# First batch's stage-1 banks emptied by two engines on opposite halves, w loaded amid x, the left-over column loaded early

## The chip, the cores and the metric

The kernel runs on one core of a Trainium2 chip. The core has TensorE (PE in the rows; its weight loads are PEld), VectorE (DVE), ScalarE (ACT), GpSimd (POOL) and SyncE (SP, which issues most DMAs). The metric is the device time of one run in microseconds (us). The time before is 1080.98 us, the median of three runs (1078.39 to 1082.65).

## The reference

`x` has 8 batches of 2496 positions of 256 channels. Each batch goes through a real FFT along the positions, a complex product with `w_r` and `w_i`, a soft threshold and an inverse FFT. The result, 19968 rows of 256, goes through a mixture of eight experts, of which each row takes one.

```python
X = np.fft.rfft(x, axis=1)
Yr = Xr @ w_r - Xi @ w_i + b_r
Yi = Xr @ w_i + Xi @ w_r + b_i
Yr = np.sign(Yr) * np.maximum(np.abs(Yr) - lam, 0.0)      # Yi alike
y = np.fft.irfft(Y, n=x.shape[1], axis=1)
# then per row: skip_score = x @ w_skip; e_idx = argmax(x @ w_gate)
y[mask] = gate_w[mask, None] * (np.maximum(xc[mask] @ w1[e], 0.0) @ w2[e])
out[do_compute] = xc + y
```

## The kernel before

2496 is 39 times 64, so the FFT is done in two stages of matrix products with constant tables. Stage 1 is the 39-point transform: for the position `n2` of 64 it multiplies 39 inputs by `fwd1`. Stage 2 (`fwd2_step`, L485) is a 64-point transform for each of 20 frequencies `k`. `mix` (L515) multiplies by w, and `inv2_step` and `out_tasks` do the way back. The main loop at L900 takes one frequency of one batch per step: 8 batches of 20 steps. In it a step of one batch's stage 2 stands beside units of the next batch's stage 1, and every instruction's place on its engine follows from the order in which the code emits it: engines take their instructions in that order, and wait on semaphores.

Products in the main loop are made of three single-pass products, so each operand is split into a high part (a ScalarE copy to fp32r: `xh`, `fh`, `wh`) and a low part (the rest, by VectorE or GpSimd: `xl`, `fl`, `wl`).

Batches 1 to 7 pass through memory between the stages: stage 1 (`a1_unit`, `a1_mm`, tile `pa`) writes `z`, then `zs` in memory, and `load_r` (L475) reads it back as `r`. Position 63 is left over by the division of 63 positions into units; it is done for three batches at a time from a small tile `xq` (`a1_left_prep`, L453).

Batch 0 takes a shorter way, `a1_first` (L393). Its `x` comes laid out as 43 groups of 128 columns (`x0`), in six DMAs of seven groups and a small one (`x_e`). TensorE multiplies each group by `fwd1` in full fp32, four groups to a PSUM bank (`pd`): 11 banks, of which six buffers exist. Every bank has 128 partitions; the lower half holds channels 0 to 127, the upper half channels 128 to 255. For each half h, ScalarE copies the first 20 frequencies (real parts) to partitions 0 to 63 of `r0`, then VectorE copies the other 19 to partitions 64 to 127 (L409, L410). `r0` is what stage 2 of batch 0 reads.

After `a1_first` come the splits of `fwd1` (L886) and of the three matrices in `wst` (w_i - w_r, w_i + w_r, w_r; L887), and then three steps of `fwd2_step` ahead of the main loop. Before everything, `spin` (L323) runs five products on zeros on TensorE.

DMAs that SP issues use eight semaphores in rotation: an issue waits until the DMA eight places earlier has landed. Their order on SP is shown with the change.

```python
            for h in range(2):                                    # L407
                rows, d = slice(64 * h, 64 * h + 64), slice(128 * h + 3 * g0, 128 * h + 3 * g0 + w)
                nc.scalar.activation(r0[0:64, :, d], src[rows, :K1, :w], AF.Copy)
                nc.vector.tensor_copy(r0[64:128, 1:, d], src[rows, K1:, :w])
```

Of the kernel before, what the change touches and what calls it, by code (L numbers as in the profile page):

```python
# [37 lines left out]
G0 = 43  # L38
# [11 lines left out]
GROUPS = ((0, 1, 2), (3, 4, 5), (6, 7))  # L50
# [245 lines left out]
def fft_and_route(tc, a, out, zs, xs, kp, pp, keep_, outer):  # L296
    nc = tc.nc
# [7 lines left out]
    KG = 5  # L305
# [30 lines left out]
    fwd2 = cp.tile([128, K1, 128], F32, name="fwd2")  # L336
# [11 lines left out]
    def setup_a():  # L348
        nc.sync.dma_start(bias[:, 0], a["b_r"].unsqueeze(0).broadcast_to((128, D)))
        nc.sync.dma_start(bi, a["b_i"].unsqueeze(0).broadcast_to((128, D)))  # L350
        nc.vector.memset(neglam, -LAM)
# [38 lines left out]
        mm(pa[:np_, :n], f1l[:np_, :np_], xh[:np_, :n], start=False, stop=True)  # L390
        return pa

    def a1_first(loads):  # L393

        at = lambda g: next((t, g - g0) for t, g0, g1 in loads if g0 <= g < g1)
        for g0 in range(0, G0, 4):
            gs = range(g0, min(g0 + 4, G0))
            w = min(3 * len(gs), 128 - 3 * g0)
            pd = bank(pp, f"pd{g0}")
            for i, g in enumerate(gs):  # L400
                t, gg = at(g)
                mm(
                    pd[:, P1 * i : P1 * i + P1], t[:, 128 * gg : 128 * gg + 128], fwd1,
                    start=True, stop=True, skip_group_check=True,
                )
            src = pd[:, : P1 * len(gs)].rearrange("p (w k) -> p k w", k=N1)
            for h in range(2):  # L407
                rows, d = slice(64 * h, 64 * h + 64), slice(128 * h + 3 * g0, 128 * h + 3 * g0 + w)
                nc.scalar.activation(r0[0:64, :, d], src[rows, :K1, :w], AF.Copy)  # L409
                nc.vector.tensor_copy(r0[64:128, 1:, d], src[rows, K1:, :w])  # L410
        for q in range(K1 // KG):
            rt[0, q] = r0[:, KG * q : KG * q + KG]

    def a1_tasks(b):

        tasks = []

        def unit(c, o, no, first, last):
            st = {}

            def prep():
                if first and (b, c) not in xraw:
                    load_x(b, c)
                st["t"] = a1_unit(b, c, o, no, xraw[b, c])

# [25 lines left out]
        return tasks

    def a1_left_prep(bs, st):  # L453
        np_ = N1 * len(bs)
        t = xp.tile([P1, D], F32, name=f"xq{bs[0]}", tag="xq", bufs=1)
        nc.sync.dma_start(t[:np_], a["xq"][bs[0] : bs[-1] + 1].rearrange("b n d -> (b n) d"))
        xh = xp.tile([P1, 2 * D], F32R, name=f"xh{bs[0]}q", tag="xh", bufs=3)
        xl = xp.tile([P1, 2 * D], F32R, name=f"xl{bs[0]}q", tag="xl", bufs=3)
        nc.scalar.activation(xh[:np_, :D], t[:np_], AF.Copy)
        nc.gpsimd.tensor_tensor(out=xl[:np_, :D], in0=t[:np_], in1=xh[:np_, :D].bitcast(F32), op=ALU.subtract)  # L460
        st["t"] = xh, xl, D
# [23 lines left out]
    def fwd2_step(b, k):  # L485
        r = rt[b, k // KG]
        kk = k % KG
        kp_ = 128 if k else 64
        pb = bank(pp, f"pb{b}_{k}")[:, : 2 * 128].rearrange("p (h c) -> p h c", h=2)
        for h in range(2):  # L490
            mm(pb[:, h], r[:kp_, kk, 128 * h : 128 * h + 128], fwd2[:kp_, k], start=True, stop=True)  # L491
        p = k // 2
        if k % 2 == 0:
            xb[b, p] = [sp.tile([128, 2, 3, 2, 64], F32R, name=f"f{n}{b}_{p}", tag="f" + n, bufs=2) for n in "hl"]
            sb[b, p] = sp.tile([128, 2, 2, 64], F32, name=f"s{b}_{p}", tag="sum", bufs=2)
        (xh, xl), s = xb[b, p], sb[b, p]
        for_k = lambda t: t[:, :, 0:2, k % 2, :]
        src = pb.rearrange("p h (c j) -> p h c j", c=2)
        nc.scalar.activation(for_k(xh), src, AF.Copy)  # L499
        im = sp.tile([128, 2, 64], F32, name=f"im{b}_{k}", tag="im", bufs=2)  # L500
        nc.scalar.activation(im, src[:, :, 1], AF.Copy)  # L501
        nc.vector.tensor_tensor(out=for_k(xl), in0=src, in1=for_k(xh).bitcast(F32), op=ALU.subtract)  # L502
        nc.vector.tensor_tensor(out=s[:, :, k % 2], in0=src[:, :, 0], in1=im, op=ALU.subtract)
        if k % 2:
            def split_sum():
                nc.scalar.activation(xh[:, :, 2], s, AF.Copy)
                nc.gpsimd.tensor_tensor(out=xl[:, :, 2], in0=s, in1=xh[:, :, 2].bitcast(F32), op=ALU.subtract)  # L507

            defer(*D_SUM, split_sum)
# [342 lines left out]
    def a1_step(q, ahead=2):  # L852
# [6 lines left out]
        if n >= ahead or not q:  # L859
            if prepped:  # L860
                prepped.pop(0)[1]()

    loads = []
    for g0, g1 in ((0, 14), (14, 28), (28, 42), (42, G0)):
        t = sp.tile([P1, CH * RW], F32, name=f"x0_{g0}", tag="row", bufs=3) if g1 < G0 else xp.tile([P1, D], F32, name="x0_e", tag="xq", bufs=1)
        n = 128 * (g1 - g0)
        for c in range(0, n, 128 * CH):
            c1 = min(c + 128 * CH, n)
            nc.sync.dma_start(t[:, c:c1], a["x0"][:, 128 * g0 + c : 128 * g0 + c1])
        loads.append((t, g0, g1))  # L870
    nc.sync.dma_start(fwd2[:, 0:KG], a["fwd2"][:, 0:KG])
    wr = wst[:, 2]
    nc.sync.dma_start(wr, a["w_r"].rearrange("(h p) e -> p h e", p=128))
    nc.sync.dma_start(wi, a["w_i"].rearrange("(h p) e -> p h e", p=128))
    load_x(1, 0)
    nc.gpsimd.tensor_tensor(out=wst[:, 0], in0=wi, in1=wr, op=ALU.subtract)
    nc.gpsimd.tensor_tensor(out=wst[:, 1], in0=wi, in1=wr, op=ALU.add)
    setup_a()
    nc.sync.dma_start(fwd2[:, KG : 2 * KG], a["fwd2"][:, KG : 2 * KG])
    load_x(1, 1)  # L880
    nc.sync.dma_start(inv2[:, 0:KG], a["inv2"][:, 0:KG])
    load_x(1, 2)
# [200 lines left out]
```

## Time and profile before

| | |
|---|---|
| median of three runs | 1080.98 us |
| the profiled execution, its own time | 1079.93 us |
| its span in the trace | 1078.2 us |
| TensorE busy | 1038.8 us, 96% of the span |
| VectorE busy | 718.6 us, 67% |
| ScalarE busy | 619.0 us, 57% |
| GpSimd busy | 437.5 us, 41% |
| moved by DMA | 132.33 MB, mean 123 GB/s |

The rows of a timeline give the start, the length (from the first to the end of the last where several are merged, with xN), the engine, the line, the operation with output and inputs, and in brackets the idle time before it and what ended it. TensorE's granted clock stands in the views by stretches as a share: 1.00 is 2.4 GHz, 0.50 is 1.2 GHz.

### The profile page before, as it was taken

The numbers are of one execution on the slowest core, as the hardware profiler recorded it, in microseconds if no ns is written. First come the engines' busy times: TensorE is split into PE (matmuls) and PEld (weight loads), VectorE is DVE, ScalarE is ACT, GpSimd is POOL, SyncE is SP. The second block draws the span as 40 slices with busy tenths as digits, with TensorE's granted clock in tenths as the row PEclk, the third lists the DMA queues.
The fourth block names the chain that finished last, engine by engine and source line by source line (L and its number), as shares of the span: only waits on it lengthen the run. The fifth ranks groups of instructions, "written<-read, shape, count | busy, mean of one in ns | idle before, by whom it ended". The sixth has DMA issues, their size and how long they took to land. (4 is left out here: it accounts for less than half of the span.)

```text
span 1078.2 us, 27343 instructions
## 1 busy us (share of the span) xinstructions
PE 1038.8 (96%) x8572; PEld 1017.0 (94%) x8572; DVE 718.6 (67%) x2025; ACT 619.0 (57%) x1811; POOL 437.5 (41%) x599
## 2 busy tenths in 40 slices
PE   7979999999999999999989989999999999999997
PEld 6879999999999999999989989999999999999997
DVE  4677787987888878789986444454545455465443
ACT  5758887788887878877875333243323343244232
POOL 1514177383665836734457522222222222222222
PEclk8989999999999999999999999999999999999999
DMA  8653656666567556463345641131413123141111
GB/s 274 187 145 85 173 147 176 181 170 183 145 166 225 138 169 167 115 180 93 115 117 146 221 114 52 39 113 47 123 39 117 46 70 96 39 130 46 39 39 40
DMA packets 83184, 132.33 MB, mean 123 GB/s; under 512 B 12504, under 2 KB 61578, under 8 KB 83080
## 3 DMA queue, kind: packets, MB, share of 16 engines
q1 hardware_dynamic: 68085, 110.45, 36.8%
q0 software_dynamic: 14864, 20.55, 6.2%
q8 instruction: 52, 0.85, 0.4%
q14 instruction: 53, 0.43, 0.1%
q10 hardware_dynamic: 130, 0.05, 0.0%
HBM read 69.77 MB, written 72.07 MB: 132 GB/s over the span
## 5 line engine op out<-in xcount | busy, mean ns | idle before, releaser
L224 ACT ACTIVATE hh<-ph 128x256 fp32r<-128x256 f32 x304 | 118.0, 388 | 289.5 <-PE ph L222 269.2
L648 POOL DMA_INDIRECT xs<-row,pos x168 | 169.1, 1007 | 62.5 <-issue 28.0
L225 DVE SCALAR_TENSOR_TENSOR hl<-ph,hh 128x256 fp32r<-128x256 f32 x304 | 128.2, 424 | 59.1 <-ACT hh L224 58.9
L545 DVE SCALAR_TENSOR_TENSOR y<-pm,rl 64x256 f32<-64x256 f32 x320 | 134.2, 419 | 4.4 <-issue 0.2
L525 PE MATMUL pm<-wh,fh 128*128 128x256 f32 x480 | 110.9, 313 | 14.9 <-DVE y L545 8.0
L507 POOL TENSOR_TENSOR fl<-s,fh 128x256 fp32r<-128x256 f32 x80 | 58.7, 734 | 162.8 <-issue 80.3
L243 DVE SCALAR_TENSOR_TENSOR ot<-pos,xres 128x256 f32<-128x256 f32 x76 | 33.3, 480 | 109.4 <-PE ph L222 95.4
L491 PE MATMUL pb<-fwd,r 128*128 128x128 f32 (+1 forms) x640 | 100.6, 281 | 4.2 <-ACT r L409 4.2
L222 PE MATMUL ph<-bxh,wb1h 128*128 128x256 f32 x352 | 98.8, 281 | 2.7 <-PEq L1079 2.7
L525 PEld LDWEIGHTS pm<-wh,fh 128*128 128x128 f32 x480 | 76.7, 193 | 23.2 <-DVE y L545 8.2
L222 PE MATMUL ph<-bxh,wb1l 128*128 128x256 f32 x352 | 98.2, 279 | 0.0
L222 PE MATMUL ph<-bxl,wb1h 128*128 128x256 f32 x352 | 98.2, 279 | 0.0
L561 PE MATMUL pi<-inv,y 128*128 128x128 f32 (+1 forms) x640 | 97.0, 274 | 0.3 <-ACT z L432 0.3
L525 PE MATMUL pm<-wh,fl 128*128 128x256 f32 x480 | 96.6, 283 | 0.5 <-DVE fl L502 0.5
L525 PE MATMUL pm<-wl,fh 128*128 128x256 f32 x480 | 96.9, 283 | 0.1
L491 PEld LDWEIGHTS pb<-fwd,r 128*128 128x128 f32 (+1 forms) x640 | 88.5, 195 | 7.8 <-ACT r L409 4.6
L499 ACT ACTIVATE fh<-pb 128x256 fp32r<-128x256 f32 x160 | 61.1, 382 | 59.2 <-PE pb L491 57.4
L256 POOL DMA_INDIRECT out<-ot,idx x78 | 78.1, 1002 | 28.6 <-issue 27.6
L382 POOL TENSOR_TENSOR xl<-xr,xh 117x512 fp32r<-117x512 f32 x63 | 81.0, 1287 | 21.1 <-ACT xh L380 20.2
L561 PEld LDWEIGHTS pi<-inv,y 128*128 128x128 f32 x640 | 84.7, 191 | 0.7 <-ACT z L432 0.5
L580 DVE TENSOR_TENSOR tl<-pt,th 117x266 fp32r<-117x266 f32 x168 | 71.2, 428 | 16.8 <-ACT th L579 16.5
L502 DVE TENSOR_TENSOR fl<-pb,fh 128x256 fp32r<-128x256 f32 x160 | 67.8, 424 | 16.9 <-ACT im L501 13.0
(222 smaller groups left out, 3189.4 us busy)
## 6 DMA issues: line engine op xcount, KB each, us to landing
out<-row SPq DMA_DIRECT2D x72, 273.0 KB
xr<-in_xc SPq DMA_DIRECT2D x21, 819.0 KB
zs<-z SPq DMA_DIRECT2D x63, 273.0 KB
r<-zs SPq DMA_DIRECT2D x49, 320.0 KB
ws<-in_moe_w SPq DMA_DIRECT2D x28, 512.0 KB
xbuf<-xs SPq DMA_DIRECT2D x41, 258.0 KB, 2.8
xs<-row,pos POOLq DMA_INDIRECT x168, 4.7
x<-in_x SPq DMA_DIRECT2D x6, 409.5 KB
```

The source lines that it names most:

```text
L222: self.nc.tensor.matmul(p, l_[:, c, fc], r_[:, c, :], start=n == 0, stop=n == 5)
L224: self.nc.scalar.activation(self.hh[:, f, :], p, AF.Relu)
L225: self.nc.vector.scalar_tensor_tensor(out=self.hl(f), in0=p, scalar=0.0, in1=self.hh[:, f, :].bitcast(F32), op0=ALU.max, op1=ALU.subtract)
L256: si = gp.indirect_dma_start(out=self.out, out_offset=bass.IndirectOffsetOnAxis(ap=self.idx[:, r : r + 1], axis=0), in_=ot[:, r, :], in_of ...
L382: eng.tensor_tensor(out=xl[:, :n], in0=v, in1=xh[:, :n].bitcast(F32), op=ALU.subtract)
L491: mm(pb[:, h], r[:kp_, kk, 128 * h : 128 * h + 128], fwd2[:kp_, k], start=True, stop=True)
L502: nc.vector.tensor_tensor(out=for_k(xl), in0=src, in1=for_k(xh).bitcast(F32), op=ALU.subtract)
L525: mm(out, flat(l_, h, j), r_[:, j, h], start=start and n == 0, stop=n == 5, skip_group_check=True)
L545: nc.vector.scalar_tensor_tensor(out=y[64 * c : 64 * c + 64], in0=t[rows, c], scalar=LAM, in1=r[rows, c], op0=ALU.add, op1=ALU.min)
L561: mm(pi[:, h, :nn], y[:, 128 * h : 128 * h + 128], inv2[:, k, :nn], start=True, stop=True)
L580: nc.vector.tensor_tensor(out=tl[:np_], in0=pt[:np_], in1=th[:np_].bitcast(F32), op=ALU.subtract)
L648: si = nc.gpsimd.indirect_dma_start(out=xs, out_offset=bass.IndirectOffsetOnAxis(ap=pos[pl, o : o + 1], axis=0), in_=row[pl, o, :], in_off ...
```

## The change

In each bank ScalarE and VectorE now start on opposite halves and then change over, so that both are at work in one bank. w is loaded after the second of the six parts of x, and xq for batches 0 to 2 behind the first loads (for the later groups one chunk earlier). `fwd1` is split before the banks. `wst` is joined amid the banks and split in three pieces (ScalarE and GpSimd): one after bank 8, two between the first steps of stage 2. Two products on zeros follow the last bank.

```diff
-    def a1_first(loads):
+    def a1_first(loads, more):
...
-            for h in range(2):
-                rows, d = slice(64 * h, 64 * h + 64), slice(128 * h + 3 * g0, 128 * h + 3 * g0 + w)
-                nc.scalar.activation(r0[0:64, :, d], src[rows, :K1, :w], AF.Copy)
-                nc.vector.tensor_copy(r0[64:128, 1:, d], src[rows, K1:, :w])
+            n = g0 // 4
+            for turn in range(2):
+                def part(h):
+                    return slice(64 * h, 64 * h + 64), slice(128 * h + 3 * g0, 128 * h + 3 * g0 + w)
+
+                rows, d = part(turn)
+                ai = nc.scalar.activation(r0[0:64, :, d], src[rows, :K1, :w], AF.Copy)
+                rows, d = part(1 - turn)
+                vi = nc.vector.tensor_copy(r0[64:128, 1:, d], src[rows, K1:, :w])
...
+            for f in more.pop(g0 // 4, ()):
+                f()
...
+                    if c == 0:
+                        for bs in GROUPS[1:]:
+                            if bs[0] == b:
+                                load_left(bs)
...
-        t = xp.tile([P1, D], F32, name=f"xq{bs[0]}", tag="xq", bufs=1)
-        nc.sync.dma_start(t[:np_], a["xq"][bs[0] : bs[-1] + 1].rearrange("b n d -> (b n) d"))
+        t = xleft.pop(bs)
...
+    f1h, f1l = split(nc, cp, fwd1, [P1, P1], "f1")
...
+    load_first(0, 14)
     wr = wst[:, 2]
     nc.sync.dma_start(wr, a["w_r"].rearrange("(h p) e -> p h e", p=128))
     nc.sync.dma_start(wi, a["w_i"].rearrange("(h p) e -> p h e", p=128))
+    load_first(14, 28)
+    load_first(28, 42)
+    load_first(42, G0)
+    nc.sync.dma_start(fwd2[:, 0:KG], a["fwd2"][:, 0:KG])
...
+    load_left(GROUPS[0])
...
-    a1_first(loads)
-    f1h, f1l = split(nc, cp, fwd1, [P1, P1], "f1")
-    wh, wl = split(nc, cp, wst, [128, 3, 2, D], "w")
+    def split_w(j):
+        nc.scalar.activation(wh[:, j], wst[:, j], AF.Copy)
+        nc.gpsimd.tensor_tensor(out=wl[:, j], in0=wst[:, j], in1=wh[:, j].bitcast(F32), op=ALU.subtract)
...
+    a1_first(loads, {5: [lambda: join_w(0, ALU.subtract), lambda: join_w(1, ALU.add)], 8: [lambda: split_w(0)]})
+    spin(2)
...
         fwd2_step(0, i)
+        if i < 2:
+            split_w(2 - i)
```

On SP, from the program's start, before (x_0, x_14, x_28 are the parts of batch 0's x, wst and wi the two matrices; `waits DMAHWn` is the semaphore of an earlier DMA in the rotation):

```order
L869 DMA x_28_107<-in_x 117x896 x2
L869 DMA x_e<-in_x 117x128
L871 DMA fwd_92<-in_fwd 128x640 [waits DMAHW0_49]
L873 DMA wst<-in_w_r 128x2x256 [waits DMAHW1_49]
L874 DMA wi<-in_w_i 128x2x256 [waits DMAHW2_49]
L316 DMA xr_0_115<-in_xc 117x1792 [waits DMAHW3_49]
L349 DMA bias<-in_b_r 128x256 [waits DMAHW4_49]
L350 DMA bi<-in_b_i 128x256 [waits DMAHW5_49]
L879 DMA fwd_92<-in_fwd 128x640 [waits DMAHW6_49]
L316 DMA xr_1_123<-in_xc 117x1792 [waits DMAHW7_49]
```

and now:

```order
L893 DMA x_0_105<-in_x 117x896 x2
L898 DMA wst<-in_w_r 128x2x256
L899 DMA wi<-in_w_i 128x2x256
L893 DMA x_14_110<-in_x 117x896 x2
L893 DMA x_28_113<-in_x 117x896
L893 DMA x_28_113<-in_x 117x896 [waits DMAHW0_49]
L893 DMA x_e<-in_x 117x128 [waits DMAHW1_49]
L903 DMA fwd_92<-in_fwd 128x640 [waits DMAHW2_49]
...
L316 DMA xr_0_122<-in_xc 117x1792 [waits DMAHW5_49]
...
L316 DMA xr_1_125<-in_xc 117x1792 [waits DMAHW7_49]
L474 DMA xq_127<-in_xq 117x256 [waits DMAHW1_49,DMAHW0_49,PE_49]
...
L316 DMA xr_2_131<-in_xc 117x1792 [waits DMAHW3_49]
```

The two w transfers stand between the second and the third part of x, and xq follows xr_1 and waits for TensorE, since it takes the buffer of x_e.

On ScalarE, the end of the banks and the first steps of stage 2 (fh and im are the copies of fwd2_step), before:

```order
L409 ACTIVATE r_89<-pd_220 64x20x8 x2
L287 ACTIVATE f1h<-fwd_87 117x117
L287 ACTIVATE wh<-wst 128x1536
L499 ACTIVATE fh_0_246<-pb_0_243 128x2x2x64
L501 ACTIVATE im_0_250<-pb_0_243 128x128
L499 ACTIVATE fh_0_246<-pb_1_254 128x2x2x64
```

and now:

```order
L413 ACTIVATE r_89<-pd_210 64x20x12 x2
L917 ACTIVATE wh<-wst 128x512
L413 ACTIVATE r_89<-pd_221 64x20x12 x2
L413 ACTIVATE r_89<-pd_230 64x20x8 x2
L521 ACTIVATE fh_0_251<-pb_0_248 128x2x2x64
L523 ACTIVATE im_0_255<-pb_0_248 128x128
L917 ACTIVATE wh<-wst 128x512
L521 ACTIVATE fh_0_251<-pb_1_261 128x2x2x64
L523 ACTIVATE im_1_265<-pb_1_261 128x128
L917 ACTIVATE wh<-wst 128x512
```

The one copy of all three matrices has become three, of which only one stands ahead of the last banks.

On GpSimd, the work around the splits, now (before, the row of `wl` isn't there: it was one instruction of 128x1536 on VectorE):

```order
L921 TENSOR_TENSOR wst<-wi,wst 128x512 x2
L918 TENSOR_TENSOR wl<-wst,wh 128x512 x3
L529 TENSOR_TENSOR fl_0_252<-s_0_253,fh_0_251 128x2x128
L382 TENSOR_TENSOR xl_0_0_292<-xr_0_122,xh_0_0_291 117x512
L529 TENSOR_TENSOR fl_1_275<-s_1_276,fh_1_274 128x2x128
L382 TENSOR_TENSOR xl_0_2_321<-xr_0_122,xh_0_2_320 117x512
```

Three low parts of w now stand ahead of the first `fl` on this engine.

## Rows read from the trace of the kernel before

**Rows 1.** The page's first part: busy time, share of the span, instructions.

```profile
PE 1038.8 (96%) x8572; PEld 1017.0 (94%) x8572; DVE 718.6 (67%) x2025; ACT 619.0 (57%) x1811; POOL 437.5 (41%) x599
```

**Rows 2.** TensorE's waits, whole span: total us, times, longest.

```profile
PE pm L525 <- DVE y L545: 8.0, 16, 1.4
...
PE pm L525 <- ACT fh L499: 5.7, 1, 5.7
PE pb L491 <- ACT r L409: 4.2, 1, 4.2
```

**Rows 3.** Timeline, batch 0's stage 1.

```profile
1.33 4.63 PE L327 MATMUL pw<-pad 128*128 128x256 f32 x10 [1.33 <-POOL pad L151]
...
5.75 9.62 PE L402 MATMUL pd<-fwd,x 117*128 117x117 f32 x84
...
7.74 0.76 ACT L409 ACTIVATE r<-pd 64x240 f32<-64x240 f32 x2 [0.46 <-DVE r L410]
8.14 0.82 DVE L410 COPY r<-pd 64x228 f32<-64x228 f32 x2 [0.43 <-ACT r L409]
8.99 0.76 ACT L409 ACTIVATE r<-pd 64x240 f32<-64x240 f32 x2 [0.49 <-DVE r L410]
...
15.21 0.39 PE L402 MATMUL pd<-fwd,x_e 117*128 117x117 f32 x2
...
20.52 0.32 DVE L410 COPY r<-pd 64x152 f32<-64x152 f32 x1 [0.37 <-ACT r L409]
```

**Rows 4.** Timeline of SP's DMA issues (start, length of the issue).

```profile
6.12 0.40 SPq L873 DMA_DIRECT2D wst<-in_w_r  x1
...
7.41 0.34 SPq L316 DMA_DIRECT2D xr<-in_xc  x1
...
12.32 0.33 SPq L879 DMA_DIRECT2D fwd<-in_fwd  x1
...
14.96 0.33 SPq L883 DMA_DIRECT2D fwd<-in_fwd  x1
```

**Rows 5.** Groups by line from 20 to 54 us: busy us, mean ns.

```profile
L382 POOL TENSOR_TENSOR xl<-xr,xh 117x512 fp32r<-117x512 f32 x9 | 11.5, 1289 | 2.7 <-ACT xh L380 2.6
L380 ACT ACTIVATE xh<-xr 117x512 fp32r<-117x512 f32 (+1 forms) x12 | 7.1, 588 | 0.0
```

**Rows 6.** Timeline, the first steps of stage 2.

```profile
22.07 0.38 ACT L499 ACTIVATE fh<-pb 128x256 fp32r<-128x256 f32 x1
22.08 1.76 DVE L288 TENSOR_TENSOR wl<-wst,wh 128x1536 fp32r<-128x1536 f32 x1 [0.93 <-ACT wh L287]
...
22.52 0.38 ACT L499 ACTIVATE fh<-pb 128x256 fp32r<-128x256 f32 x1
...
25.85 0.73 POOL L507 TENSOR_TENSOR fl<-s,fh 128x256 fp32r<-128x256 f32 x1 [8.28 <-ACT fh L506]
...
28.36 0.38 ACT L499 ACTIVATE fh<-pb 128x256 fp32r<-128x256 f32 x1 [2.07 <-PE pb L491]
...
30.09 0.74 POOL L507 TENSOR_TENSOR fl<-s,fh 128x256 fp32r<-128x256 f32 x1 [2.28 <-ACT fh L506]
...
32.14 0.49 PE L389 MATMUL pa<-xl,f1h 117*117 117x512 f32 x1 [0.28 <-POOL xl L382]
```

**Rows 7.** Stretches: length, busy time of each engine (instructions), granted clock, DMA.

```profile
28.00:30.00 2.00, 2.00 (x13) 2.00 (x12) 0.95 (x3) 0.95 (x4) 0.00 (x0) 0.55 0.82 316
...
62.00:64.00 2.00, 2.00 (x12) 2.00 (x12) 1.01 (x3) 0.00 (x0) 0.00 (x0) 0.51 0.78 222
```

**Rows 8.** Timeline around the first use of xq.

```profile
53.48 0.61 PE L561 MATMUL pi<-inv,y 128*128 128x128 f32 x4
56.79 0.42 ACT L459 ACTIVATE xh0q<-xq 117x256 fp32r<-117x256 f32 x1 [6.09 <-DMA xq<-in_xq]
...
59.84 0.77 PE L525 MATMUL pm<-wh,fh 128*128 128x256 f32 x2 [5.75 <-ACT fh L499]
```

**Rows 9.** Timeline of SP's issues, batch 1's first reload.

```profile
71.28 0.52 SPq L478 DMA_DIRECT2D r<-zs  x1
```

**Rows 10.** Timeline of TensorE, batch 1's first step of stage 2.

```profile
78.75 0.71 PE L491 MATMUL pb<-fwd,r 64*128 64x128 f32 x4
```

More of the change, by code (lines that the diff above doesn't have):

```diff
@@ L406, in a1_first @@
             src = pd[:, : P1 * len(gs)].rearrange("p (w k) -> p k w", k=N1)
-            for h in range(2):
-                rows, d = slice(64 * h, 64 * h + 64), slice(128 * h + 3 * g0, 128 * h + 3 * g0 + w)
-                nc.scalar.activation(r0[0:64, :, d], src[rows, :K1, :w], AF.Copy)
-                nc.vector.tensor_copy(r0[64:128, 1:, d], src[rows, K1:, :w])
+            n = g0 // 4
[6 more added lines that the diff above has]
+                vi = nc.vector.tensor_copy(r0[64:128, 1:, d], src[rows, K1:, :w])
+                for di, own, other in ((ai, "a", "v"), (vi, "v", "a")):
+                    tc.add_to_no_dep_group(f"r0{own}{n}{turn}", di.ins)
+                    tc.declare_no_dep(di.ins, group=f"r0{other}{n}{turn}", reason="other partitions of the bank and of r0")
+                    if n:
+                        for t in range(2):
+                            tc.declare_no_dep(di.ins, group=f"r0{other}{n - 1}{t}", reason="another bank and other partitions of r0")
+            for f in more.pop(g0 // 4, ()):
+                f()
         for q in range(K1 // KG):
@@ L451, in a1_tasks, with load_left @@
         return tasks
+    xleft = {}
+    def load_left(bs):
+        t = xleft[bs] = xp.tile([P1, D], F32, name=f"xq{bs[0]}", tag="xq", bufs=1)
+        nc.sync.dma_start(t[: N1 * len(bs)], a["xq"][bs[0] : bs[-1] + 1].rearrange("b n d -> (b n) d"))
     def a1_left_prep(bs, st):
         np_ = N1 * len(bs)
-        t = xp.tile([P1, D], F32, name=f"xq{bs[0]}", tag="xq", bufs=1)
-        nc.sync.dma_start(t[:np_], a["xq"][bs[0] : bs[-1] + 1].rearrange("b n d -> (b n) d"))
+        t = xleft.pop(bs)
         xh = xp.tile([P1, 2 * D], F32R, name=f"xh{bs[0]}q", tag="xh", bufs=3)
@@ L861, in a1_step, with load_first @@
                 prepped.pop(0)[1]()
+    f1h, f1l = split(nc, cp, fwd1, [P1, P1], "f1")
     loads = []
-    for g0, g1 in ((0, 14), (14, 28), (28, 42), (42, G0)):
+    def load_first(g0, g1):
         t = sp.tile([P1, CH * RW], F32, name=f"x0_{g0}", tag="row", bufs=3) if g1 < G0 else xp.tile([P1, D], F32, name="x0_e", tag="xq", bufs=1)
@@ L870, in fft_and_route @@
         loads.append((t, g0, g1))
-    nc.sync.dma_start(fwd2[:, 0:KG], a["fwd2"][:, 0:KG])
+    load_first(0, 14)
     wr = wst[:, 2]
@@ L874, in fft_and_route, with join_w @@
     nc.sync.dma_start(wi, a["w_i"].rearrange("(h p) e -> p h e", p=128))
+    load_first(14, 28)
+    load_first(28, 42)
+    load_first(42, G0)
+    nc.sync.dma_start(fwd2[:, 0:KG], a["fwd2"][:, 0:KG])
+    setup_a()
     load_x(1, 0)
-    nc.gpsimd.tensor_tensor(out=wst[:, 0], in0=wi, in1=wr, op=ALU.subtract)
-    nc.gpsimd.tensor_tensor(out=wst[:, 1], in0=wi, in1=wr, op=ALU.add)
-    setup_a()
     nc.sync.dma_start(fwd2[:, KG : 2 * KG], a["fwd2"][:, KG : 2 * KG])
     load_x(1, 1)
+    load_left(GROUPS[0])
     nc.sync.dma_start(inv2[:, 0:KG], a["inv2"][:, 0:KG])
+    nc.sync.dma_start(fwd2[:, 2 * KG :], a["fwd2"][:, 2 * KG :])
     load_x(1, 2)
-    nc.sync.dma_start(fwd2[:, 2 * KG :], a["fwd2"][:, 2 * KG :])
     nc.sync.dma_start(inv2[:, KG:], a["inv2"][:, KG:])
-    a1_first(loads)
-    f1h, f1l = split(nc, cp, fwd1, [P1, P1], "f1")
-    wh, wl = split(nc, cp, wst, [128, 3, 2, D], "w")
+    wh = cp.tile([128, 3, 2, D], F32R, name="wh")
+    wl = cp.tile([128, 3, 2, D], F32R, name="wl")
+    def split_w(j):
+        nc.scalar.activation(wh[:, j], wst[:, j], AF.Copy)
+        nc.gpsimd.tensor_tensor(out=wl[:, j], in0=wst[:, j], in1=wh[:, j].bitcast(F32), op=ALU.subtract)
+    def join_w(j, op):
+        nc.gpsimd.tensor_tensor(out=wst[:, j], in0=wi, in1=wr, op=op)
+    a1_first(loads, {5: [lambda: join_w(0, ALU.subtract), lambda: join_w(1, ALU.add)], 8: [lambda: split_w(0)]})
+    spin(2)
     a1q = a1_tasks(1)
```

## The prediction

> **What bounds the kernel now.** I read four views in this order: the page's busy shares, TensorE's waits over the whole span, the timeline at the places that these waits name, and the granted clock there. TensorE is busy 96% of the span, the next engine 67% [rows 1], so what counts is when TensorE stands still or runs at half its clock. Its waits are few [rows 2]: 16 short ones for `y`, spread over the loop, and two single long ones, 4.2 us for ScalarE's copy into `r` and 5.7 us for ScalarE's `fh`. Both long ones lie in the first 60 us, and the change works on both. After 60 us I find no wait that would swallow time won earlier, so what is won there should reach the end.
>
> The first place is batch 0's stage 1. ScalarE and VectorE take turns [rows 3]: ScalarE starts a pair of copies at 7.74 and the next pair at 8.99, so a bank costs 1.25 us, while ScalarE works only 0.76 us of it and VectorE 0.82. Eleven banks end at 20.84 (20.52 + 0.32). TensorE ended its products at 15.60 and stood still. Then the split of all of w lies on the path: `fh` of stage 2 starts only at 22.07, behind ScalarE's copy of w, and VectorE spends 1.76 us on its low part [rows 6]. From 20 us on TensorE runs at half its clock: the share is 0.55 at 28 to 30 us [rows 7], after 4.2 us of standing still.
>
> The second place is `xq`. ScalarE waits 6.09 us for it, to 56.79; TensorE's last product before is the group at 53.48 (to 54.09), its next one at 59.84 [rows 8]. It again runs at 1.2 GHz afterwards: 0.51 at 62 to 64 us [rows 7].
>
> **The change part by part.**
>
> *Arrival of x.* SP's issue times show when transfers landed, since an issue waits for the one eight places earlier. Part 3 of x landed by 7.41 and part 6 by 12.32, that is 1.64 us a part; everything up to w landed by 14.96 [rows 4]. With both w transfers put behind part 2, I take one part's time, 1.65 us, for their 524 KB (two matrices of 256x256 in fp32; a part of 117x896 has 419 KB). Part 6 then lands at 13.95 and x_e at about 14.3. The bounds are no delay (12.3, if the queues serve both side by side) and 2.6 us (all of w and the table behind x_e, 14.96 less 12.32).
>
> *Stage 1.* TensorE does 42 groups in 9.62 us, with its waits, so 0.23 us a group at most [rows 3]; the seven groups of part 6 and x_e end at 15.8. With both engines in one bank each turn lasts as long as VectorE's copy, 0.41 us, so a bank takes 0.82 us, below the 0.94 us in which its x arrives (1.64 us times 4/7). So x sets the pace, not the copies. Bank 8 has its x when the first group of part 6 is done, 14.2, and is empty at 15.05. ScalarE's first piece of w is next: 128x512, priced by its copies of 117x512, 0.59 us [rows 5], to 15.65. Bank 9 takes 0.8 us and the short bank 10 two copies of 0.32 us: `r` is complete at 17.1 instead of 20.84. That is 3.7 us. The bounds are 15.5 (x not delayed) and 21.4 (halves of one bank don't go together after all, 20.84 + 0.59).
>
> The Trainium skill, "PSUM — Partial Sum Buffer", section "PSUM bank collisions raise a hardware error", says that two engines must not be in one bank and one group of 32 partitions together, while different groups of a bank may be used at the same time. No row here shows two engines in one bank: the copies that overlap at 8.14 belong to neighbouring banks. By that rule the opposite halves go together and the sum is as above; were a bank's halves to shut each other out, a bank would stay at 1.25 us.
>
> *The two products on zeros.* Five took 4.63 us at the start [rows 3], so two cost 1.85 us at that pace. They start at 15.8, end by 17.65 at the latest, and lie in the time in which TensorE waits for `r` anyway. If they run as fast as the rest of the stage they end before 17.1. Their cost is 0 to 0.5 us; I take 0.
>
> *The split of w.* ScalarE's `fh` of step 0 needs TensorE's first products after 17.1: 17.45. Pairs of `fh` and `im` start 0.45 us apart (22.07, 22.52) [rows 6], and two pieces of w stand between: second piece done 18.5, third 19.55. GpSimd makes a low part of 512 columns in 1.29 us [rows 5]: the first is done beside the last banks, the second runs 18.55 to 19.8, the third to 21.1. Then the first `fl` can start, at 21.1 instead of 25.85 [rows 6]: 4.75 us earlier. VectorE has 1.76 us less to do there, which hides behind GpSimd.
>
> *The next steps.* After `fl` (0.73) TensorE needs 0.7 us until the next pair of stage 2's products is there: `fh` at 22.6 instead of 28.36. From that `fh` to the second `fl` it was 1.73 us (28.36 to 30.09) [rows 6] on ScalarE and VectorE alone, so 24.35. After 0.74 the low part of x follows, 1.29 us, and TensorE's product that waited for it until 32.14 starts at 26.4. The gain stands at 5.7 us. It is more than 4.75 because TensorE no longer stretches the steps at 1.2 GHz. From there on TensorE was full before as it will be after. The bounds are 4.1 us (half the clock again) and 7 us (GpSimd without a gap from 18.55: two low parts of w, two `fl`, two low parts of x, 6.6 us, to 25.2).
>
> *xq for batches 0 to 2.* It is issued when TensorE has done x_e, 15.8, behind the parts of x of batch 1 and the tables that SP issued ahead of it, and needed past 45 us: the wait goes. What is late next is ScalarE's own work: it starts at 50.7 instead of 56.79, and the `fh` that TensorE awaited at 59.84 is ready about 6.1 us earlier, at 53.7, so before TensorE's work ends at 54.09. I take 5.65 us (59.84 to 54.2). TensorE also keeps 2.4 GHz: from 59.84 to about 64 us it ran at half, 4.2 us that shrink to 2.1. Together 7.7 us. Bounds: 5.6 (the clock falls anyway) and 8.2. The other two `xq` loads kept only ScalarE waiting; TensorE's waits name neither [rows 2], so they bring 0.
>
> *SP's queue.* The load of `xq` holds SP until 15.8, where the issues behind it (the tables from `inv2` on, the third part of batch 1's x) waited on landings anyway; this is hidden by the loads under way. The bytes are the same.
>
> *Sum.* 5.7 + 7.7 = 13.4 us off the profiled execution's 1079.93 (span 1078.2): 1066.5. The median of the runs is 1.05 above it, so I forecast 1067.5 as a median.
>
> **The rivals.**
>
> *Half clock at the start again.* The work that filled TensorE at 28 to 30 us at 0.55 [rows 7] fills little over half the time at 1.00, and so it is from 17 to 26 us: some 5.5 us of work with gaps. The trace has no such stretch at 2.4 GHz: it shows that the clock fell after waits of 4.2 and 5.7 us and rose after about 10 and 4 us of nearly unbroken work. If it falls here, stage 1's gain is 4.1 instead of 5.7: 1069. The skill's page "TensorE: Matmul & The Clock Gate", section "A second HAM failure mode: psum-queue depth-cycling", says that short idles between groups of products can make the clock go back and forth; by it this rival is the likelier one. The waits of up to 1.4 us for `y` [rows 2] that left the clock up in the loop speak against it. 15%.
>
> *A transfer becomes the wait.* Batch 1's `r` was issued at 71.28 [rows 9], when its rows in memory had landed, and first used at 78.75 [rows 10]. The use moves by 7.7 us against `xq`'s wait, the issue by only about 6.2, since the stores keep their length. So 1.5 us go of the 7.5 between them, of which the landing takes a part that no row shows. It should hold; if it doesn't, or if a table or x of batch 1 is late at 30 to 45 us, 2 to 4 us are lost: 1070.5. 10%.
>
> *The banks don't go together,* or x comes so late that it is the same. `r` at 21.4, the split still beside other work: stage 1 brings about 1 instead of 5.7, `xq` 7.7: 1072.3. For it: each second turn still waits for the other engine. Against: both copies are of nearly equal length. 7%.
>
> *Slower: the clock stays at half through batch 0.* With more but shorter gaps TensorE would work at 1.2 GHz up to the end of batch 1's stage 1. Every microsecond of full-speed work then costs one more. It decides from 27 us on: 13.4 us of such work, 27 us at half, undo the gain, and half clock from 27 to 65 us costs 19 more: 1086.5. Against: at half clock the work of 17 to 26 us fills that time, and nearly unbroken work brought the clock back at 30 and at 64 us. 2%.
>
> **How the numbers follow.** Forecast 63%, from 1064 to 1070 (sums of the bounds, and 1 us for the runs' own spread); the rivals 15, 10, 7 and 2%; a gain beyond 16 us 3%. The range takes in the first three rivals and leaves out the rest: 1063.5 to 1073. A measurement of this kernel can tell about 0.5%, 5.4 us, from no change: faster means under 1075.6, which every case but the slower one and a part of the third reaches: 95%. No change 3%, slower 2%.
>
> **What would show it.** Right: ScalarE's and VectorE's copies start together in a bank; `r` complete near 17 us; the first `fl` on GpSimd near 21; granted clock 1.00 throughout 17 to 30 us; no wait of ScalarE for `xq`, and TensorE without a gap over 1 us from 27 us on. Wrong: part 6 of x after 15 us, a stretch at 0.50, TensorE waiting for batch 1's `r`, or a gain that is there at 60 us and gone at 100.

## The result and the profile after

The changed kernel takes 1067.80 us (median of 4 runs, 1066.72 to 1071.07), the kernel before 1081.67 on the same chip (4 runs). The ratio is 0.988, with a 95% interval of 0.9865 to 0.9894: by it 13.0 us less, between 11.5 and 14.6. The profiled executions are 13.2 us apart (1079.93 and 1066.72).

The first part of the page after answers to [rows 1], and TensorE's waits to [rows 2]:

```profile
PE 1033.2 (97%) x8576; PEld 1010.9 (95%) x8576; DVE 716.4 (67%) x2024; ACT 620.0 (58%) x1813; POOL 441.6 (41%) x602
```

```profile
PE pm L547 <- DVE y L567: 8.5, 17, 1.4
...
PE pd L402 <- DMA x<-in_x: 1.1, 1, 1.1
...
PE pm L547 <- POOL fl L529: 0.8, 1, 0.8
```

The short waits for `y` are as they were. Both long single waits are gone; in their place are one of 1.1 us for x and one of 0.8 us for GpSimd's `fl`.

The timeline of batch 0's stage 1 and the first steps of stage 2, after, beside [rows 3, 6]:

```profile
6.77 2.59 ACT L413 ACTIVATE r<-pd 64x240 f32<-64x240 f32 x6 [1.29 <-PE pd L402]
6.77 2.61 DVE L415 COPY r<-pd 64x228 f32<-64x228 f32 x6 [0.97 <-PE pd L402]
...
10.03 0.33 SPq L316 DMA_DIRECT2D xr<-in_xc  x1
10.06 7.23 PE L402 MATMUL pd<-fwd,x 117*128 117x117 f32 x56 [1.09 <-DMA x<-in_x]
...
14.90 0.80 ACT L413 ACTIVATE r<-pd 64x240 f32<-64x240 f32 x2 [0.35 <-PE pd L402]
14.90 0.82 DVE L415 COPY r<-pd 64x228 f32<-64x228 f32 x2 [0.33 <-PE pd L402]
...
17.13 0.39 PE L402 MATMUL pd<-fwd,x_e 117*128 117x117 f32 x2
...
17.35 1.04 PE L327 MATMUL pw<-pad 128*128 128x256 f32 x4
...
17.73 1.08 DVE L415 COPY r<-pd 64x228 f32<-64x228 f32 x3 [0.45 <-ACT r L413]
...
22.99 0.72 POOL L529 TENSOR_TENSOR fl<-s,fh 128x256 fp32r<-128x256 f32 x1
...
26.49 0.74 POOL L529 TENSOR_TENSOR fl<-s,fh 128x256 fp32r<-128x256 f32 x1 [1.54 <-ACT fh L528]
...
28.52 0.49 PE L389 MATMUL pa<-xl,f1h 117*117 117x512 f32 x1 [0.68 <-POOL xl L382]
```

ScalarE and VectorE start together at 6.77 and empty three banks in 2.6 us, 0.87 us a bank instead of 1.25. Then TensorE waits for part 3 of x until 10.06 (SP's issue at 10.03 waited for the same part), so the stage ends late all the same: x_e's product is 1.9 us later than before, and `r` is complete at 18.81 instead of 20.84. TensorE's product that waited for the second low part of x until 32.14 starts at 28.52.

Around the use of `xq` and after it, beside [rows 8, 9], ScalarE, TensorE and SP of the changed kernel:

```profile
47.35 0.46 ACT L481 ACTIVATE xh0q<-xq 117x256 fp32r<-117x256 f32 x1
```

```profile
60.12 0.47 PE L547 MATMUL pm<-wh,fh 128*128 128x256 f32 x2 [0.43 <-DVE y L567]
```

```profile
63.56 0.52 SPq L500 DMA_DIRECT2D r<-zs  x1
```

```profile
67.84 0.71 PE L513 MATMUL pb<-fwd,r 64*128 64x128 f32 x4
```

ScalarE doesn't wait for `xq`. TensorE's short wait at 60.12 is the one that ended at 71.00 before. Batch 1's reload is issued at 63.56 instead of 71.28 and first used at 67.84 instead of 78.75 [rows 9, 10], and TensorE doesn't wait for it.

The granted clock by stretches, beside [rows 7]:

```profile
22.00:24.00 2.00, 0.96 (x6) 0.76 (x7) 0.50 (x2) 0.78 (x2) 2.00 (x3) 1.00 0.99 233
24.00:26.00 2.00, 1.93 (x17) 1.74 (x16) 1.09 (x4) 0.56 (x3) 0.95 (x1) 1.00 1.07 264
...
28.00:30.00 2.00, 1.48 (x10) 1.38 (x11) 0.79 (x2) 1.85 (x4) 1.76 (x2) 1.00 0.86 256
```

It stays at 2.4 GHz although TensorE is busy only 0.96 of 2 us at 22 to 24.

Places that can be found in both traces show where the 13.3 us of the span come from (times in us):

| place | before | after | gain so far |
|---|---|---|---|
| first product of the inverse (`pi`) | 36.14 | 32.46 | 3.7 |
| end of a wait for `y` | 71.00 | 60.12 | 10.9 |
| SP issues a store of results | 153.87 | 142.94 | 10.9 |
| another, past the second xq | 221.87 | 210.15 | 11.7 |
| another, past the third xq | 425.34 | 413.45 | 11.9 |
| last product of the inverse | 556.5 | 544.5 | 12.0 |
| end of the span | 1078.2 | 1064.9 | 13.3 |

So stage 1 gives 3.7 us, the first `xq` 7.2, the second and third 0.8 and 0.2, and 1.3 come after the inverse FFT has ended, where nothing was changed. The experiments test this account. The first four and the last three of them ran where the kernel before takes 1111.5 to 1112.8 us, the other four where it takes 1081.5; each ratio is to the kernel before on the same chip, and so ratios and places up to 230 us are compared.

### The profile page after: what moved, and what is told of

The parts are those of the page before. It is cut to its first block, busy times and chain, and to the rows that moved or that the text cites. A ratio compares the mean times of both kernels' runs of the same rounds, so it can differ in the third digit from the quotient of the medians.

```text
span 1064.9 us, 27356 instructions
## 1 busy us (share of the span) xinstructions
PE 1033.2 (97%) x8576; PEld 1010.9 (95%) x8576; DVE 716.4 (67%) x2024; ACT 620.0 (58%) x1813; POOL 441.6 (41%) x602
## 5 line engine op out<-in xcount | busy, mean ns | idle before, releaser
L513 PE MATMUL pb<-fwd,r 128*128 128x128 f32 (+1 forms) x640 | 98.0, 276 | 0.1
L513 PEld LDWEIGHTS pb<-fwd,r 128*128 128x128 f32 (+1 forms) x640 | 86.2, 190 | 3.6 <-ACT r L413 0.5
L602 DVE TENSOR_TENSOR tl<-pt,th 117x266 fp32r<-117x266 f32 x168 | 71.1, 428 | 17.9 <-ACT th L601 17.8
L222 PE MATMUL ph<-bxh,wa1h 128*128 128x256 f32 x256 | 72.2, 282 | 4.9 <-PEq L1118 4.8
```

Of the source, the lines that this page charges most:

```text
L222: self.nc.tensor.matmul(p, l_[:, c, fc], r_[:, c, :], start=n == 0, stop=n == 5)
L602: nc.vector.tensor_tensor(out=tl[:np_], in0=pt[:np_], in1=th[:np_].bitcast(F32), op=ALU.subtract)
```

## The experiments

**xq alone** (the kernel before with the three early loads):

```diff
     load_x(1, 1)
+    load_left(GROUPS[0])
     nc.sync.dma_start(inv2[:, 0:KG], a["inv2"][:, 0:KG])
...
+                    if c == 0:
+                        for bs in GROUPS[1:]:
+                            if bs[0] == b:
+                                load_left(bs)
```

> The kernel before with one part of the change: the three left-over columns xq are loaded early (for batches 0 to 2 behind the second part of batch 1's x, for the later groups one chunk ahead); banks, w and the splits as before. My theory, from the two traces: xq's early load is worth 7.3 us by the 60th us and 0.8 to 1.0 us more near the second and third group (at 178 to 190 and 382 to 392 us before). So the first inverse product stays at 36 us, TensorE's wait for y at 71.0 moves to about 63.7, the last inverse product from 556.5 to about 548.3, the time is 8 us shorter: about 1073. Rival A: only the first of the three loads counts, and the later 0.8 us came from the shift of everything: 7.3 us, last inverse product at 549.2. Rival B: xq behind SP's wait for TensorE delays the tables, and 1 to 3 us are lost again at 30 to 45 us.

Measured: ratio 0.9919 (0.9897 to 0.9940), 9.0 us. The first inverse product is at 36.2, the wait for `y` ends at 63.89, and the stores of 153.87 and 221.87 come at 146.75 and 214.01: 7.1 us for the first load, 0.7 for the second. Both are close to what my theory had; nothing is lost to the tables (rival B).

**xq late** (the changed kernel without `load_left`, the DMA back in `a1_left_prep`):

```diff
-                    if c == 0:
-                        for bs in GROUPS[1:]:
-                            if bs[0] == b:
-                                load_left(bs)
...
-        t = xleft.pop(bs)
+        t = xp.tile([P1, D], F32, name=f"xq{bs[0]}", tag="xq", bufs=1)
+        nc.sync.dma_start(t[:np_], a["xq"][bs[0] : bs[-1] + 1].rearrange("b n d -> (b n) d"))
...
-    load_left(GROUPS[0])
```

> The changed kernel with xq loaded as before, when its first use is at hand; the rest is changed. My theory: only stage 1's 3.6 us are left (first inverse product at 32.5), and the waits for xq are back, about 6 us of ScalarE near 47 to 53 us with TensorE at half clock behind it; time 3.6 us shorter than before, about 1077.5. Rival A: the gains don't add, since the earlier start meets the same transfers: under 2 us. Rival B: stage 1 is worth more than its trace says (as forecast, 5.7 us): about 1075.5.

Measured: ratio 0.9965 (0.9950 to 0.9980), 3.9 us. The trace has ScalarE's and TensorE's waits for it:

```profile
54.66 0.42 ACT L478 ACTIVATE xh0q<-xq 117x256 fp32r<-117x256 f32 x1 [8.23 <-DMA xq<-in_xq]
...
57.70 0.76 PE L544 MATMUL pm<-wh,fh 128*128 128x256 f32 x2 [7.87 <-ACT fh L518]
```

The first inverse product is at 31.9, 4.3 us early, but the wait for `xq` has grown from 6.09 to 8.23 us [rows 8], and at the wait for `y` (69.03) only 2.0 us are left. An earlier start met a transfer that did not come as much earlier. So the parts don't add at this place (rival A): 7.1 and 2.0 alone, 10.9 together. In the time the two ratios still make up the whole within their intervals: 3.9 us (2.2 to 5.6) for this kernel, while its trace shows 2.0 at 71 us and 1.8 at 222 us. Where the other 2 us would come from isn't shown.

**Same half** (both engines in one half after the other, the rest changed):

```diff
-                rows, d = part(1 - turn)
                 vi = nc.vector.tensor_copy(r0[64:128, 1:, d], src[rows, K1:, :w])
-                for di, own, other in ((ai, "a", "v"), (vi, "v", "a")):
+                for di, own, other in ():
```

The last two lines empty the loop that declares the two engines' copies free of each other.

> The changed kernel with ScalarE and VectorE in one half of a bank after the other, as before; the loads, xq and the splits changed. My theory: by turns a bank costs 1.25 us, so eleven banks from 6.8 us and the first piece of w end near 21.0 instead of 18.8; first inverse product about 2 us later than in the changed kernel (34.5 instead of 32.5), time about 2 us over it, 1070. Rival: x arrives at 1 us a bank and sets the pace, so the opposite halves bring nothing: 32.5 and 1067.8.

Measured: ratio 0.9897 (0.9873 to 0.9921); first inverse product at 36.1, 3.6 us after the changed kernel's, the wait for `y` at 63.73. That is more than I expected, and the trace names two reasons. x_e's product came 0.7 us later, and TensorE waited and lost its clock (timeline of TensorE, then stretches):

```profile
21.04 3.37 PE L512 MATMUL pb<-fwd,r 64*128 64x128 f32 x11 [1.98 <-ACT r L413]
```

```profile
20.00:22.00 2.00, 0.96 (x3) 0.68 (x4) 1.17 (x4) 0.96 (x3) 0.79 (x1) 0.74 1.07 304
22.00:24.00 2.00, 2.00 (x9) 1.77 (x10) 1.03 (x4) 1.27 (x4) 0.20 (x1) 0.50 1.09 252
```

**No products on zeros:**

```diff
-    spin(2)
```

> The changed kernel without the two products on zeros behind the last bank. My theory: TensorE stands still for only about 1.5 us there, so the clock stays at 1.00 and the first inverse product stays at 32.5, time within 0.3 us. Rival (the one of the prediction): with the gap the clock falls to 0.50 between 17 and 30 us, and the first inverse product comes 1 to 2 us later: 1069.

Measured: ratio 0.9889 (0.9866 to 0.9913), as the changed kernel's within the intervals. But the clock did fall, after waits of 0.95 and 0.34 us:

```profile
18.16 1.97 PE L513 MATMUL pb<-fwd,r 64*128 64x128 f32 x12 [0.95 <-ACT r L413]
20.47 0.58 PE L547 MATMUL pm<-wh,fh 128*128 128x256 f32 x2 [0.34 <-ACT fh L521]
```

```profile
22.00:24.00 2.00, 1.64 (x6) 1.35 (x7) 0.20 (x2) 0.63 (x1) 1.95 (x3) 0.50 1.00 236
```

The rival is right on the clock. Its price is seen when the arrival of x is taken out, in the table below: 0.9 us.

**The changed kernel again**, beside the next three:

> The changed kernel itself, beside the others on one chip. First inverse product at 32.5 us, TensorE's wait for y at 60.1, ratio to the kernel before 0.988 as in its own runs (0.9865 to 0.9894). If the ratio is different by more than the interval, part of the gain belongs to a chip and not to the change.

Measured: 1067.34 us, ratio 0.9873 (0.9853 to 0.9893), as expected. The places are not: in its trace x came sooner (the issue on SP waits for part 3 of x):

```profile
9.29 0.33 SPq L316 DMA_DIRECT2D xr<-in_xc  x1
...
15.66 0.39 PE L402 MATMUL pd<-fwd,x_e 117*128 117x117 f32 x2
...
21.54 0.73 POOL L529 TENSOR_TENSOR fl<-s,fh 128x256 fp32r<-128x256 f32 x1
...
27.08 0.49 PE L389 MATMUL pa<-xl,f1h 117*117 117x512 f32 x1 [0.68 <-POOL xl L382]
```

The first inverse product is at 31.0, and the wait for `y` ends at 58.69. One kernel's stage 1 thus differs by 1.5 us between two executions, all of it in the arrival of x, and 1.4 us are left of it at 413 us (a store at 412.05 instead of 413.45): what is won early does last. From x_e's product to the first inverse product it is the same to 0.1 us (starts of both, in us):

| | x_e's product | first inverse product | between | clock fell in between |
|---|---|---|---|---|
| before; xq alone | 15.21; 15.84 | 36.1; 36.2 | 20.9; 20.4 | yes |
| changed | 17.13 | 32.5 | 15.3 | no |
| changed again | 15.66 | 31.0 | 15.4 | no |
| xq late | 16.51 | 31.9 | 15.4 | no |
| only the first xq early | 18.30 | 33.7 | 15.4 | no |
| no products on zeros | 16.83 | 33.0 | 16.2 | yes |
| same half | 17.80 | 36.1 | 18.3 | yes |
| same half, six on zeros | 17.12 | 35.0 | 17.8 | no |
| split whole | 16.15 | 32.7 | 16.5 | yes |
| w behind x | 15.28 | 31.5 | 16.2 | yes |
| w behind x, low parts on VectorE | 15.54 | 31.2 | 15.6 | no |
| low parts on VectorE, x of batch 1 first | 16.77 | 31.4 | 14.7 | no |

**w behind x:**

```diff
     load_first(0, 14)
-    nc.sync.dma_start(wr, a["w_r"].rearrange("(h p) e -> p h e", p=128))
-    nc.sync.dma_start(wi, a["w_i"].rearrange("(h p) e -> p h e", p=128))
...
     nc.sync.dma_start(fwd2[:, 0:KG], a["fwd2"][:, 0:KG])
+    nc.sync.dma_start(wr, a["w_r"].rearrange("(h p) e -> p h e", p=128))
+    nc.sync.dma_start(wi, a["w_i"].rearrange("(h p) e -> p h e", p=128))
...
-    a1_first(loads, {5: [lambda: join_w(0, ALU.subtract), lambda: join_w(1, ALU.add)], 8: [lambda: split_w(0)]})
+    a1_first(loads, {8: [lambda: join_w(0, ALU.subtract), lambda: join_w(1, ALU.add)]})
     spin(2)
+    split_w(0)
```

> The changed kernel with w loaded behind x, x_e and the first table, as before, and all three splits of w behind the banks; the joins of w after bank 8. My theory (w amid x delays x by 2.6 us, and this is the term that the forecast mis-sized): part 6 of x lands near 12.5 instead of 15.5, r is complete near 16.8 instead of 18.8, GpSimd joins w from 15 us and is through its three low parts at 21.4, the first fl starts at 21.4 instead of 23.0; first inverse product at 31, 1.5 us before the changed kernel's 32.5. Rival: the start is bound by GpSimd and w, not by x: w late means joins late, first fl at 23 or after, no gain or 1 us lost.

Measured: 1069.3 us, ratio 0.9888 (0.9869 to 0.9908), not told apart from the changed kernel's 0.9873. x came sooner (x_e's product at 15.28) and the first `fl` began at 21.47, as expected, but the first inverse product came at 31.5 instead of 31. The rest was lost one step on, to the first part of batch 1's x, which now stands behind w (ScalarE); beside it the clock was at 0.50 for 3.4 us, after TensorE had waited 1.41 us for that `fl`:

```profile
23.23 0.63 ACT L380 ACTIVATE xh<-xr 117x512 fp32r<-117x512 f32 x1 [3.19 <-DMA xr<-in_xc]
```

So the theory holds up to the first `fl`; behind it another transfer becomes the bound, and the gain in time can't be told, as the rival had it for another reason.

**w behind x, two low parts on VectorE:**

```diff
-        nc.gpsimd.tensor_tensor(out=wl[:, j], in0=wst[:, j], in1=wh[:, j].bitcast(F32), op=ALU.subtract)
+        (nc.vector if j else nc.gpsimd).tensor_tensor(out=wl[:, j], in0=wst[:, j], in1=wh[:, j].bitcast(F32), op=ALU.subtract)
```

> As the one with w behind x, and the low parts of the second and third piece of w on VectorE instead of GpSimd (before, VectorE took 1.76 us for all three, so about 0.6 us each against 1.27). My theory: GpSimd is free at 18.8, the first fl waits only for ScalarE's copy at about 20.5; first inverse product at 30.3. Rival: VectorE's two pieces delay its own fl and s by 0.6 to 1.2 us and with them the next steps: no better than 31.

Measured: 1067.25 us, ratio 0.9861 (0.9840 to 0.9882); first inverse product at 31.2, not the 30.3 of my theory, so the rival is right. The wait for batch 1's x is 2.0 us here. In time no gain can be told.

**Only the first xq early** (`load_left` for the later groups back at their first use):

```diff
-                    if c == 0:
-                        for bs in GROUPS[1:]:
-                            if bs[0] == b:
-                                load_left(bs)
...
+        if bs not in xleft:
+            load_left(bs)
         t = xleft.pop(bs)
```

> The changed kernel with only the first group's xq loaded early; the two later groups as before. My theory (the 0.8 us that the gain grew by between 154 and 222 us came from the second load, 0.2 from the third): ScalarE waits again 2 to 3 us for each, the store of results that the changed kernel issues at 210 us comes 0.8 us later, the time is 1 us longer. Rival: TensorE has work in hand there, and the growth came from elsewhere: no difference at 210 and 540 us.

Measured: ratio 0.9902 (0.9882 to 0.9922), by it 3.1 us over the changed kernel in the same comparison, with intervals that overlap. In the trace ScalarE waits 6.2 us for the two loads, and TensorE with it (waits of TensorE, 150 to 200 us):

```profile
PE pi L581 <- ACT z L445: 1.4, 1, 1.4
```

The store that the changed kernel issues at 142.94 comes at 144.16, that of 210.15 at 213.22: 1.85 us lost in between. Past the third load, from 345.42 to 413.45, another 0.8 are lost (348.61 to 417.41). So the growth past 154 us belongs to the later loads, as I had it, and more than the 0.8 and 0.2 us that the two first traces showed.

**Same half with six products on zeros:**

```diff
-    spin(2)
+    spin(6)
```

> The kernel with both engines in one half of a bank after the other, with six products on zeros behind the last bank instead of two. x's arrival differs between executions, so I measure from TensorE's last product of x_e to the first inverse product: 15.4 us in four executions with opposite halves and two products on zeros, 18.3 us with the same half (where the granted clock was 0.50 for 6.8 us). My theory: about 2 us of these 2.9 are the copies by turns and 0.8 to 1 the clock, so with the clock held up it is 17.3 to 17.6 us. Rival: the clock costs nothing there, since ScalarE, VectorE and GpSimd set the pace of these steps: 18.3 again with granted clock 1.00.

Measured: ratio 0.9927 (0.9899 to 0.9956). The clock stayed at 1.00, and the stretch is 17.8 us. Of the 2.9 us that the same half costs, 2.5 are the copies by turns and 0.4 the clock. It lies between theory and rival.

**Split whole:**

```diff
-    a1_first(loads, {5: [lambda: join_w(0, ALU.subtract), lambda: join_w(1, ALU.add)], 8: [lambda: split_w(0)]})
+    a1_first(loads, {5: [lambda: join_w(0, ALU.subtract), lambda: join_w(1, ALU.add)],})
     spin(2)
+    nc.scalar.activation(wh, wst, AF.Copy)
+    nc.vector.tensor_tensor(out=wl, in0=wst, in1=wh.bitcast(F32), op=ALU.subtract)
...
-        if i < 2:
-            split_w(2 - i)
```

> The changed kernel with the split of w as before, whole and behind the banks: one copy of 1536 columns on ScalarE, its low part on VectorE. From the last product of x_e to the first inverse product it is 15.4 us with the split in pieces. My theory: ScalarE's copy (1.47) stands ahead of the first fh and VectorE's low part (1.76) ahead of the first fl, but GpSimd has its 3.8 us of low parts off, so the first fl on GpSimd comes 0.7 to 1 us later: 16.2 us, and TensorE stands still for 2 us, so the clock may fall, which adds up to 0.8. Rival: as GpSimd is the bound in the pieces, the whole split is no worse: 15.4.

Measured: ratio 0.9898 (0.9871 to 0.9926); the stretch is 16.5 us, 1.2 us longer, and the clock fell for 3.4 us. That lies within the theory's 16.2 to 17.0.

**Low parts on VectorE, batch 1's x ahead of the bias loads:**

```diff
-    setup_a()
     load_x(1, 0)
+    setup_a()
```

with VectorE's low parts as above.

> The changed kernel with two steps more: the low parts of the second and third piece of w on VectorE, and the first part of batch 1's x issued ahead of the two bias loads (its landing kept ScalarE waiting 0.46 us in the changed kernel, 3.2 us with w behind x). My theory: first fl on GpSimd 0.8 us earlier, from x_e to the first inverse product 14.6 instead of 15.4 us; in time 0.8 us, less than can be told from none. Rival: VectorE's two pieces take it from its own fl and s, no change at 15.4.

Measured: ratio 0.9877 (0.9856 to 0.9899); the stretch is 14.7 us, 0.7 less than the changed kernel's, where 0.8 were expected. In time it can't be told from the changed kernel. No version has been shown to beat it.

**The end of the span.** The 1.3 us that came after 545 us were not tried by a kernel of their own, but the traces from where the kernel before takes about 1081 us bear on them. From the last inverse product to the end it is 521.7 us before, 520.4 and 521.1 in the changed kernel's two executions, and 521.7, 524.1 and 522.7 in three edited ones that leave that part as it is. Where the first blocks of experts wait, the clock falls in some executions: before, and with two low parts on VectorE, by stretches:

```profile
626.00:630.00 4.00, 0.81 (x7) 0.64 (x7) 0.05 (x1) 0.00 (x0) 0.00 (x0) 1.00 0.00 0
630.00:634.00 4.00, 4.00 (x22) 4.00 (x23) 3.44 (x9) 2.27 (x6) 2.32 (x5) 0.57 0.20 34
```

```profile
616.00:620.00 4.00, 1.25 (x6) 1.28 (x7) 0.81 (x3) 0.00 (x0) 0.46 (x3) 0.70 0.01 4
620.00:624.00 4.00, 4.00 (x20) 4.00 (x20) 3.16 (x8) 2.71 (x6) 2.31 (x4) 0.50 0.28 73
```

In the changed kernel's two executions it didn't fall there. All three edited kernels do it too. So I count the 1.3 us as chance of that execution and not as the change's; six executions argue for it, no experiment shows it.

## Why the prediction was right

The time, 1067.8, is 0.3 us from the forecast, and the mechanisms are the forecast's: the two long waits go, the clock stays up, the rest of the kernel keeps what was won. But the closeness is in part luck: in the profiled execution stage 1 brought 2.0 us less than forecast and the first `xq` 0.5 less, the later two 1.0 more and the end of the span 1.3 more.

*Arrival of x: mis-sized.* The forecast had x_e's product end at 15.8; it ended at 17.5, and at 16.0 in the second execution. SP's issues wait for the landings: part 3 of x had landed by 7.41 before [rows 4], and by 10.03 and 9.29 in the changed kernel's two executions, 2.6 and 1.9 us later. The forecast took 1.65 us for both w transfers, with 2.6 as its bound. Over all executions part 3 landed by 9.9 on average with w amid x (nine, 9.29 to 10.72) and by 8.0 with w behind (four, 7.41 to 8.78), so w costs about 2.0 us, and the trace that the forecast started from had the earliest landing of the four. At x_e's product less is left: it starts between 15.66 and 18.30 with w amid x, 16.9 on average (the latest one after half the clock in stage 1), and between 15.21 and 15.84 with w behind, 15.5 on average. With w behind x, TensorE itself is late: part 6 had landed by 12.32 before, and x_e's product started only at 15.21. So the forecast of 15.8 was missed by 1.7 us in the profiled execution and by 0.2 in the second.

*Banks by opposite halves: right.* 0.87 us a bank against 0.82. By the Trainium skill, "PSUM — Partial Sum Buffer", section "PSUM bank collisions raise a hardware error", different groups of 32 partitions of a bank may be used at the same time. The trace agrees: both engines are in one bank from 6.77 on, and a bank's two copies take 0.80 us on ScalarE and 0.82 on VectorE side by side, against 0.76 and 0.82 by turns [rows 3]. Undoing this costs 2.5 us at a held clock, the largest part of stage 1's gain.

*Split of w and the next steps: right, and late by x's delay.* From `r` complete to the first `fl` the forecast had 4.0 us, the trace 4.2; from there to the second `fl` 3.25 against 3.5; from that to the waiting product 2.05 against 2.03. So stage 1 brought 3.7 us in the profiled execution and 5.1 in the second, where 5.7 were forecast. The early split of `fwd1`, whose copy took ScalarE 0.29 us behind the last bank before, was not tried alone.

*Products on zeros: right to cost nothing, but their use was missed.* They filled 1.0 us while TensorE waited. Without them the clock falls and 0.9 us go. So the rival of the half clock was nearer than its 15%, at about half of its price (1.6 us). The Trainium skill, "TensorE: Matmul & The Clock Gate", section "A second HAM failure mode: psum-queue depth-cycling", tells of short idles between groups of products that make the clock go back and forth. Once the products on zeros were left out, the trace shows one fall, after waits of 0.95 and 0.34 us, and one rise within 7 us.

*The first xq: right,* 7.2 against 7.7 us, 7.1 when alone.

*The later two: wrong.* They were put at 0, because the list of TensorE's waits over the span named neither. They brought 1.0 us, and cost 2.6 when they alone are put back. ScalarE's stall reached TensorE as a wait of another name, for ScalarE's `z`: 1.4 us when they alone are put back, and already 0.3 us in the kernel before, where ScalarE had waited 2.56 us for the second `xq`:

```profile
187.23 0.42 ACT L459 ACTIVATE xh3q<-xq 117x256 fp32r<-117x256 f32 x1 [2.56 <-DMA xq<-in_xq]
...
188.19 0.71 PE L561 MATMUL pi<-inv,y 128*128 128x128 f32 x4 [0.33 <-ACT z L432]
```

A list by pairs doesn't name a wait's origin.

*The sum.* Forecast 5.7 + 7.7; measured 3.7 + 7.2 + 1.0 + 1.3, the last by the argument above not the change's. The forecast's range, 1064 to 1070, is not what it names as its source: the bounds of the two parts, 4.1 to 7 and 5.6 to 8.2 us, with 1 us at either end give 1064.8 to 1072.3.

*The rivals.* No transfer took the place of the waits in the changed kernel beyond 1.1 us for x. In the version with w behind x one did, 3.2 us. For batch 1's `r` the forecast had about 6 us left between issue and use; it came to 4.3 (63.56 to 67.84), and still nothing waited. The slower rival did not come: wherever the clock fell in the first 30 us of a kernel with the new stage 1, it was back within 7 us.

## What to carry to other kernels

Where two engines empty one accumulator bank by turns, start them on opposite halves: it gave 2.5 us over eleven banks here. Where transfers set the pace of a start, moving one ahead moves another back, so measure from the first use of the last input, or its spread hides what an edit did. A small load that is issued only when its use is near can be late however small it is: `xq`, 117 KB, was issued at 49.72 before, behind three stores and a part of x, and used at 56.79, which kept ScalarE waiting 6 us, and 8 us once the rest was faster.

## What the runs showed of the hardware

The clock fell after a wait of 1.98 us that followed two products on zeros (same half) and after waits of 0.95 and 0.34 us (no products on zeros), while it stayed up through 0.96 us of work in 2 us in the changed kernel. In one execution of nine with w amid x (only the first xq early) it fell in stage 1 itself, after TensorE had waited 1.09 us for x; in another (same half with six products on zeros) it stayed up after such a wait of 1.49 us. So the length of the last wait doesn't decide alone. The one where it fell:

```profile
8.00:10.00 2.00, 0.91 (x8) 0.73 (x8) 1.08 (x3) 1.01 (x3) 1.43 (x2) 1.00 0.98 307
...
12.00:14.00 2.00, 2.00 (x10) 2.00 (x11) 0.85 (x3) 0.80 (x3) 0.00 (x0) 0.51 1.00 283
```

VectorE's low part of 128x512 took 1.20 us beside GpSimd's and 0.67 alone (w behind x, low parts on VectorE; with batch 1's x first, where GpSimd is idle nearly throughout, 0.68 twice):

```profile
18.08 1.27 POOL L918 TENSOR_TENSOR wl<-wst,wh 128x512 fp32r<-128x512 f32 x1
18.70 1.20 DVE L918 TENSOR_TENSOR wl<-wst,wh 128x512 fp32r<-128x512 f32 x1
...
20.36 0.67 DVE L918 TENSOR_TENSOR wl<-wst,wh 128x512 fp32r<-128x512 f32 x1
```

The Trainium skill, "SBUF — State Buffer", section "Who interferes with whom", says that a VectorE instruction with two inputs in SBUF contends with a GpSimd instruction that reads SBUF; these rows agree.
